# A decode step of attention and MLP on one core: x's load on another queue, two groups of loads merged, products in pairs, one semaphore for two copies

## The chip, the cores and the metric

The kernel runs on one core of one Trainium2 chip. The metric is the device time of one execution in microseconds (us). Three runs of the kernel before took 100.2, 100.45 and 100.91 us, median 100.45. Besides these there is one profiled execution.

## The reference

One token (x is one row of 1024 numbers, bf16) goes through a layernorm, and its result through two branches, which are added to x. Cut to what matters:

```python
xn = layernorm(x)
# branch A: attention of one query over the last W = 4096 positions of the cache
q = (xn @ wq).reshape(32 heads, 128)             # wq: 1024 x 4096
k, v = k_cache[:, -W:, :], v_cache[:, -W:, :]    # 4 heads x 4096 x 128, each serves 8 query heads
p = softmax(q @ k.T * 128**-0.5)
A = (p @ v).reshape(4096) @ wo                   # wo: 4096 x 1024
# branch B: an MLP with a layernorm of its own
y = layernorm(xn)
B = gelu(y @ w1 + b1) @ w2 + b2                  # w1: 1024 x 3584, w2: 3584 x 1024
out = x + A + B
```

In bf16 wq, wo are 8 MB each, w1 and w2 7 MB each, and the used parts of K and V 4 MB each: some 40 MB are read for one row of output.

## The kernel before, in words

All weights stream from HBM through four large SBUF buffers (slot 0 to 3, 32 KB in each of 128 partitions), in this order: wq's first row, K, the rest of wq, b1 and b2, w1, V, w2, wo. A "row" of a weight here is one step of the contraction: a weight of 1024 or 4096 or 3584 rows is laid over 128 partitions, and row c holds one 1024 (or 4096, 3584) long line for each partition. wo has 32 such rows of 2 KB per partition.

The order of the work is written by hand as a list of operations (class Plan). Each names an engine, what it reads and what it writes; `emit` (L27) works out from these keys which operation must wait for which, gives each engine's waited-for operations ticks of that engine's semaphore, gives every load a semaphore of its own, and puts the instructions out. SyncE (SP) issues all loads of the plan in list order, so a load that has to wait for its buffer holds back the ones behind it.

Before the plan come a few loads outside it (L205): SyncE issues wq's first row (1 MB) and then K in four loads, one for each of the four heads (`load_k`, L199; head g goes to partitions g, g+4, g+8, ...), and ACT issues the load of x, 2 KB, as a 32x32 tile x32. `tc.close()` then ends this part with a barrier over all engines (L209).

Then, in the order in which TensorE (PE) works:

- x: GpSimd (POOL) makes a mask (spread, L260, L261), and four small products with it bring x into a column layout (L284). The layernorms are short VectorE (DVE) operations, with two sums on TensorE (L286 to L316).
- K is transposed in 32x32 blocks on VectorE (four transposes, L340, which read all four heads), and copied into place by ACT (L345) and VectorE (L349).
- q = xn @ wq (L375 and helper L233), scores, w1's products, the softmax.
- V's products in a loop (L501), whose output is scaled and turned into o8, one column for each row of wo (L517 to L544).
- w2's rows go partly to VectorE (running sums in run, L488), and rows 21 to 27 to TensorE (`bulk_rows`, L528, into sc_ps).
- wo's rows 0 to 15 are loaded in two loads (L511, slot 0) and multiplied row by row: each row needs one weight load and two products of 512 columns, all into PSUM partition 0 of sc_ps. wo's rows 16 to 31 are loaded in pieces of 8, 4, 2, 1 and 1 rows (L513, slot 2). Rows 16 to 23 are multiplied in pairs (groups=2): two rows at once, in two column groups of the array, into partitions 0 and 32 of sc_ps.
- VectorE adds sc_ps to run (two halves, L556), while rows 24 to 31 go into another PSUM buffer (L567), to which run is added by small products (L572).
- VectorE and ACT each copy one part of the result (L575, L576), and SyncE and ACT each store one half (L578, L579). Each store needs both copies: it waits for VectorE's semaphore and for ACT's.

The rule that says for each row of wo which load it needs, and the calls that multiply them:

```python
return wo_t[i][:, r, :], f"wo0{r // 8 * 8}" if i == 0 else f"wo1{max(a for a in cuts if a <= r)}"
...
bulk_rows(list(range(16)), wo_row, ocol, "o8")
bulk_rows(list(range(16, NB)), wo_row, ocol, "o8", last=True, groups=2)
```

Of the kernel before, what the change touches and what calls it, by code (L numbers as in the profile page):

```python
# [14 lines left out]
class Plan:  # L15
# [8 lines left out]

        self.ops.append((eng, fn, tuple(r), tuple(w), dma, tuple(over)))

    def emit(self, done):  # L27
        nc, ops = self.nc, self.ops
        writer, readers, deps = {}, {}, []
        for n, (eng, fn, r, w, dma, over) in enumerate(ops):  # L30
# [26 lines left out]
        for n, (eng, fn, r, w, dma, _) in enumerate(ops):  # L57
            c, mine = clock[eng], []
# [13 lines left out]
        wanted = {m for mine in waits for m in mine if ops[m][4] is None}  # L72
        wanted.update(m for m in range(len(ops)) if m in done)
        sems = {e: nc.alloc_semaphore(f"{e}_count") for e in ("pe", "pool", "sp")}
        used, ends = list(sems.values()), []
        value, ticks = {}, {e: 0 for e in self.engines}
# [2 lines left out]
            ends.append(sems[e])  # L79
        left = nc.alloc_semaphore("left")  # L80
        ends.append(left)
        for n in done:
            value[n] = (nc.alloc_semaphore(f"dma{n}"), 16)
        for n, (eng, fn, r, w, dma, _) in enumerate(ops):
            if dma is not None:
                if n in done:
                    continue
                value[n] = (nc.alloc_semaphore(f"dma{n}") if dma is True else dma, 16)
                used.append(value[n][0])
            elif n in wanted:  # L90
                ticks[eng] += 1
                value[n] = (sems[eng], ticks[eng])

# [25 lines left out]
        for n in done:  # L119
            s, v = value[n]  # L120
# [18 lines left out]
def kernel(  # L139
# [32 lines left out]
    NB = 24  # L172
# [13 lines left out]
    slot = [sb(f"slot{i}", [P, 16384], BF16) for i in range(4)]  # L186
# [5 lines left out]

    x_flat = A_x.rearrange("a b d -> (a b d)")
    k_sb, kt_scr = slot[0], slot[3]
    k_sem = [nc.alloc_semaphore(f"k{g}") for g in range(Hkv)]
    wq_v = A_wq.rearrange("(p c) n -> p c n", p=P)
    wq_sem = nc.alloc_semaphore("wq0")

    def load_k(g):  # L199
        return nc.sync.dma_start(out=k_sb[g:P - Hkv + g + 1:Hkv, :],  # L200
                                 in_=A_k_cache[0, g, Sk - W:Sk, :].rearrange("(r c) d -> r (c d)", r=P // Hkv))

    x32 = sb("x32", [Hq, Hq], BF16)
    x_sem = nc.alloc_semaphore("x32")
    for i, sem in [(nc.sync.dma_start(out=slot[1][:, 0:NQ], in_=wq_v[:, 0, :]), wq_sem)] + [(load_k(g), k_sem[g]) for g in range(Hkv)] + [(nc.scalar.dma_start(out=x32, in_=x_flat.rearrange("(a j) -> a j", a=Hq)), x_sem)]:  # L205
        i.then_inc(sem, 16)
        tc.no_tile_sem_insts.add(i.ins.name)
    tc.close()
# [2 lines left out]
    plan = Plan(nc)  # L211
    pe, dve, act, pool, sp = nc.tensor, nc.vector, nc.scalar, nc.gpsimd, nc.sync

    def op(eng, fn, r=(), w=()):
        plan.add(eng, fn, r, w)

    def dma(eng, out_ap, in_ap, r=(), w=(), over=()):
        q = plan.engines[eng]
        plan.add(eng, lambda: q.dma_start(out=out_ap, in_=in_ap), r, w, True, over)  # L219
# [19 lines left out]
        op("pe", lambda: pe.matmul(out_ap, lhsT=w_ap, rhs=x_ap, start=start, stop=stop, tile_position=pos), r, w)  # L239

    plan.add("sp", lambda: None, (), ("wq0",), wq_sem)
    for g in range(Hkv):
        plan.add("sp", lambda: None, (), (f"k{g}",), k_sem[g])
    plan.add("act", lambda: None, (), ("x32",), x_sem)

    w1_v = B_w1.rearrange("(p c) n -> p c n", p=P)
    w2_v = B_w2.rearrange("(p c) n -> p c n", p=P)
# [89 lines left out]
    T5 = kt_scr.rearrange("p (s c a j) -> p s c a j", s=NS, a=4, j=32)  # L337
    T3 = kt_scr.rearrange("p (c a j) -> p c a j", a=4, j=32)
    for s in range(NS):
        op("dve", lambda s=s: dve.transpose(out=scr[:, s, :], in_=k2[:, s, :]), ("k0", "k1", "k2", "k3", "slot0"), (f"scr{s}",))  # L340
    pairs = [(R, Cd) for R in range(4) for Cd in range(4)]
    ACT_PAIRS = 6
    for s0, s1 in ((0, 1), (1, 2), (2, 4)):
# [39 lines left out]
    for c in (2, 3):  # L383
        for t in range(4):
            ldw(xw[:, 96 + P * c:97 + P * c], (0, 32 * t), ("xw",))
        for b in range(2):
            for t in range(4):
                j = 2 * (3 - t) + b
# [119 lines left out]
    op("pe", lambda: pe_loop("v", (NCH - 2) // UV, v_rows), v_in, ())  # L508
    op("pe", lambda: v_step(NCH - 1, False, True), v_in, ("qo",))
    wo_t = [slot[s].rearrange("p (r n) -> p r n", r=16) for s in (0, 2)]  # L510
    for a in (0, 8):  # L511
        dma("sp", wo_t[0][:, a:a + 8, :], wo_v[:, a:a + 8, :], (), (f"wo0{a}",), ("slot0",))
    cuts = [0, 8, 12, 14, 15, 16]  # L513
    for a, b in zip(cuts[:-1], cuts[1:]):
        dma("sp", wo_t[1][:, a:b, :], wo_v[:, 16 + a:16 + b, :], (), (f"wo1{a}",), ("slot2",))
# [31 lines left out]

    def wo_row(c):
        i, r = divmod(c, 16)
        return wo_t[i][:, r, :], f"wo0{r // 8 * 8}" if i == 0 else f"wo1{max(a for a in cuts if a <= r)}"  # L550

    ocol = lambda c: o8[:, c:c + 1]
    bulk_rows(list(range(16)), wo_row, ocol, "o8")
    bulk_rows(list(range(16, NB)), wo_row, ocol, "o8", last=True, groups=2)
    for half in range(2):
        op("dve", lambda half=half: dve.tensor_tensor(out=run[0][0:33, 512 * half:512 * half + 512], in0=bulk[:, half, :],  # L556
                                                      in1=run[0][0:33, 512 * half:512 * half + 512], op=ALU.add), ("bulk", "run0"), (f"sum{half}",))
# [19 lines left out]
    out_v = out.rearrange("a b (t s n) -> t (a b) s n", t=2, s=16)  # L577
    dma("sp", out_v[0], res[0:1, :].rearrange("a (s n) -> a s n", s=16), ("res_a", "res_b"), ("out0",))  # L578
    dma("act", out_v[1], res[32:33, :].rearrange("a (s n) -> a s n", s=16), ("res_a", "res_b"), ("out1",))  # L579
    plan.emit([len(plan.ops) - 2, len(plan.ops) - 1])  # L580


# [28 lines left out]
```

## Time and profile before

| what | value |
|---|---|
| three runs | 100.2, 100.45, 100.91 us |
| profiled execution, its own time | 99.88 us |
| its span, first to last instruction | 98.6 us |
| mean granted TensorE clock | 0.879 |
| busy: PE, DVE, ACT, POOL | 59.4, 73.9, 30.8, 10.0 us |
| SyncE's load queue: packets, MB | 3082, 39.86 |
| x's load on ACT's queue: issued, us to landing | 0.80, 3.4 |
| K's four loads: issued | 1.26, 1.84, 2.47, 3.10 |
| K's four loads: us to landing | 6.9, 8.7, 10.6, 12.3 |
| first transpose of K on VectorE starts | 15.48 |
| wo's rows 0 to 7 and 8 to 15: issued | 58.27, 58.64 |
| wo's rows 0 to 7 and 8 to 15: us to landing | 23.2, 27.8 |
| result copies start: DVE, ACT | 96.73, 96.83 |
| stores are issued: SP, ACT | 97.25, 97.27 |

How to read it: times inside the profile count from the span's start. "Issued" is when the engine's queue took the load, and "us to landing" counts from there until its semaphore was full, so a long time to landing is mostly a place far back in the queue. Engine names in the profile's lines: PE is TensorE, PEld its weight loads, DVE VectorE, POOL GpSimd, SP SyncE; L233 and L219 are lines of helpers that issue most products and all of the plan's loads. In lines of the timeline the bracket at the end is the idle time before the group and what ended it.

### The profile page before, as it was taken

How to read it: one execution, taken by the hardware profiler on the slowest of the kernel's cores; microseconds unless marked ns; L12 is line 12 of the kernel's file. 1: busy time of each engine (PE TensorE's matmuls, PEld its weight loads, DVE VectorE, ACT ScalarE, POOL GpSimd, SP SyncE). 2: the span in 40 equal slices, each digit the busy share in tenths (PEclk: the TensorE clock that was granted, in tenths of full speed). 3: DMA queues.
4: the chain of work that ended last, by engine and by line, in shares of the span. 5: the costliest groups of instructions: out<-in, count | busy, mean ns of one | idle time of the engine just before them, and what ended most of it. 6: DMA issues, size and time to landing. Idle time of an engine off the chain costs nothing.

```text
span 98.6 us, 958 instructions
## 1 busy us (share of the span) xinstructions
PE 59.4 (60%) x323; PEld 16.6 (17%) x220; DVE 73.9 (75%) x75; ACT 30.8 (31%) x29; POOL 10.0 (10%) x22
## 2 busy tenths in 40 slices
PE   0032040599400699940899566887671899995792
PEld 0022000123000234400212111212211111111130
DVE  0023777999999999999103685999999999999231
ACT  0050000089999899992002095000000000000001
POOL 0072580000000670000000000000000000000000
PEclk9999999999998558995559999579998558999999
DMA  2999979999999899899799999999998999999970
GB/s 60 443 442 439 479 316 475 425 525 425 425 425 404 384 407 512 384 407 512 311 425 425 425 437 434 419 425 459 430 489 371 432 425 445 432 425 382 401 288 1
DMA packets 3133, 39.86 MB, mean 404 GB/s; under 512 B 439, under 2 KB 445, under 8 KB 829
## 3 DMA queue, kind: packets, MB, share of 16 engines
q1 hardware_dynamic: 3082, 39.86, 95.5%
q10 hardware_dynamic: 50, 0.00, 0.0%
q14 instruction: 1, 0.00, 0.0%
HBM read 39.86 MB, written 0.00 MB: 404 GB/s over the span
## 4 chain that ended last, share of the span: by engine, by line
DMA 64%; PE 25%; issue 4%; SPq 1%; DVE 0%
DMA slot<-in_A_wq_dram 27%; DMA slot<-in_A_wo_dram 20%; DMA slot<-in_A_v_cache_dram 17%; PE qo_ps L501 11%; PE acc L375 10%; PE acc L233 2%; PE acc L239 1%; SPq L219 1%; DVE res L575 0%
## 5 line engine op out<-in xcount | busy, mean ns | idle before, releaser
L345 ACT COPY kT<-slot 32x1024 bf16<-32x1024 bf16 (+1 forms) x18 | 23.9, 1327 | 14.2 <-DVE slot L340 14.0
L488 DVE SCALAR_TENSOR_TENSOR run<-slot,hTf,run 128x1024 f32<-128x1024 bf16 x20 | 24.2, 1270 | 0.0
L375 PE MATMUL acc<-slot,xw 128*128 x48 | 16.1, 514 | 11.6 <-DMA slot<-in_A_wq_dram 11.6
L340 DVE STREAM_TRANSPOSE slot<-slot 128x4096 bf16<-128x4096 bf16 x4 | 17.4, 4413 | 1.1 <-DMA slot<-in_A_k_cache_dram 1.1
L501 PE MATMUL qo_ps<-slot,eTb 128*128 (+1 forms) x32 | 11.3, 436 | 4.2 <-issue 2.9
L349 DVE COPY kT<-slot 32x4096 bf16<-32x4096 bf16 x10 | 13.2, 1316 | 0.2
L233 PE MATMUL sc_ps<-slot,o 128*1 128x512 bf16 x48 | 9.1, 379 | 1.6 <-DMA slot<-in_A_wo_dram 1.6
L375 PEld LDWEIGHTS acc<-slot,xw 128*128 x48 | 5.7, 118 | 22.7 <-issue 20.2
L576 ACT CAST res<-acc 33x224 bf16<-33x224 f32 x1 | 0.3, 339 | 20.4 <-PE acc L233 20.4
L233 PE MATMUL sc_ps<-slot,hT 128*1 128x512 bf16 x14 | 6.0, 618 | 0.5 <-DMA slot<-in_B_w_dram 0.5
L233 PE MATMUL sc_ps<-kT,qm 128*32 128x512 bf16 x32 | 5.7, 914 | 0.3 <-DVE qm L422 0.3
L501 PEld LDWEIGHTS qo_ps<-slot,eTb 128*128 (+1 forms) x32 | 3.1, 98 | 12.1 <-issue 8.7
L544 ACT CAST o<-misc 128x32 bf16<-128x32 f32 x1 | 0.2, 187 | 14.6 <-PE misc L239 14.6
L434 DVE COPY sc<-sc_ps 128x512 f32<-128x512 f32 x1 | 0.7, 692 | 5.3 <-PE sc_ps L233 5.3
L225 PEld LDWEIGHTS <-o 128*1 128x1 bf16 x40 | 2.4, 85 | 11.6 <-issue 10.9
L239 PE MATMUL misc<-x,spread 32*128 32x8 bf16 x4 | 0.3, 168 | 6.2 <-POOL spread L261 6.2
L239 PE MATMUL acc<-spread,qm 32*128 32x512 bf16 x4 | 1.6, 497 | 3.7 <-POOL qm L321 3.7
L255 DVE MEMSET mhalf<- 128x1 f32 x1 | 0.1, 59 | 5.0 <-PEq L209 5.0
L233 PE MATMUL acc<-slot,yT 128*1 128x448 bf16 x64 | 3.5, 353 | 0.0
L433 ACT COPY sc<-sc_ps 128x512 f32<-128x512 f32 x1 | 0.6, 591 | 8.4 <-PE sc_ps L233 8.4
L239 PE MATMUL qo_ps<-selq,q_sb 128*128 128x4 bf16 x8 | 0.4, 169 | 4.0 <-DVE q_sb L394 4.0
L257 ACT ACT_TABLE_LOAD x1 | 1.3, 1283 | 4.8 <-PEq L209 4.8
(88 smaller groups left out, 48.1 us busy)
## 6 DMA issues: line engine op xcount, KB each, us to landing
slot<-in_B_w_dram SPq DMA_DIRECT2D x3, 3584.0 KB, 16.6
slot<-in_A_wo_dram SPq DMA_DIRECT2D x3, 2048.0 KB, 23.2
slot<-in_A_k_cache_dram SPq DMA_DIRECT2D x4, 1024.0 KB, 9.6
slot<-in_A_wq_dram SPq DMA_DIRECT2D x1, 4096.0 KB, 26.9
slot<-in_A_v_cache_dram SPq DMA_DIRECT2D x1, 4096.0 KB, 16.5
slot<-in_A_wq_dram SPq DMA_DIRECT2D x2, 1024.0 KB, 9.1
slot<-in_A_wq_dram SPq DMA_DIRECT2D x1, 2048.0 KB, 17.7
slot<-in_B_w_dram SPq DMA_DIRECT2D x1, 2048.0 KB, 21.5
```

The costliest lines, as they stand in the source:

```text
L219: plan.add(eng, lambda: q.dma_start(out=out_ap, in_=in_ap), r, w, True, over)
L225: return pe.add_instruction(mybir.InstLdweights(name=nc.get_next_instruction_name(), engine=i.engine, tile_size=(P, 32), tile_position=pos ...
L233: return pe.add_instruction(mybir.InstMatmult(name=nc.get_next_instruction_name(), engine=i.engine, start_tensor_calc=start, stop_tensor_c ...
L239: op("pe", lambda: pe.matmul(out_ap, lhsT=w_ap, rhs=x_ap, start=start, stop=stop, tile_position=pos), r, w)
L257: op("act", lambda: act.activation(out=dummy[:, 0:1], in_=mhalf[0:1, 0:1], func=ACT.Exp), ("mhalf",), ("act_warm",))
L340: op("dve", lambda s=s: dve.transpose(out=scr[:, s, :], in_=k2[:, s, :]), ("k0", "k1", "k2", "k3", "slot0"), (f"scr{s}",))
L345: op("act", lambda s0=s0, s1=s1, R=R, Cd=Cd: act.copy(out=kT[32 * Cd:32 * Cd + 32, R, s0:s1, :].rearrange("p s (c j) -> p (s c) j", j=32), ...
L349: op("dve", lambda R=R, Cd=Cd: dve.tensor_copy(out=kT[32 * Cd:32 * Cd + 32, R, :, :].rearrange("p s (c j) -> p (s c) j", j=32), in_=T3[32 ...
L375: pe.matmul(acc2[:, b, :], lhsT=xw[:, bass.ds(32 * n + 512 * i, P)], rhs=slot[1 + i][:, bass.ds(1024 * n + 512 * b, 512)], start=False, st ...
L434: op("dve", lambda: dve.tensor_copy(out=sc[:, 0:512], in_=sc_ps[:, 0, :]), ("sc0",), ("scs0",))
L488: op("dve", lambda: dve.scalar_tensor_tensor(out=t, in0=wap, scalar=hTf[:, c:c + 1], in1=t, op0=ALU.mult, op1=ALU.add), (key, "hTf", f"run ...
L501: return pe.matmul(qo_ps, lhsT=cols, rhs=v4[:, :, c, :], start=first, stop=last)
```

## The change

Four edits.

- The load of x is issued by SyncE, after wq's first row and ahead of K, and no longer by ACT.
- K is loaded by one load of 128 rows of 32 KB in place of four loads of 32 such rows. The layout in SBUF is the same: partition 4r + g holds piece r of head g. The transposes wait for one semaphore.
- wo's rows 0 to 15 come in one load of 32 KB per partition in place of two of 16 KB, and their products are made in pairs, in one run with those of rows 16 to 23. The weight loads and products are as many as before. All of rows 0 to 15 wait for the one load.
- The two result copies add to one new semaphore, "copied", and both stores wait for it to reach 2, in place of a wait for VectorE's and one for ACT's.

```diff
-    def emit(self, done):
+    def emit(self, done, last):
...
+        copied = nc.alloc_semaphore("copied")
+        ends.append(copied)
+        for n in last:
+            value[n] = (copied, len(last))
...
-            elif n in wanted:
+            elif n in wanted and n not in last:
...
-    k_sem = [nc.alloc_semaphore(f"k{g}") for g in range(Hkv)]
+    k_sem = nc.alloc_semaphore("k")
...
-    def load_k(g):
-        return nc.sync.dma_start(out=k_sb[g:P - Hkv + g + 1:Hkv, :],
-                                 in_=A_k_cache[0, g, Sk - W:Sk, :].rearrange("(r c) d -> r (c d)", r=P // Hkv))
+    k_rows = A_k_cache[0, :, Sk - W:Sk, :].rearrange("g (r c) d -> r g (c d)", r=P // Hkv)
...
-    for i, sem in [(nc.sync.dma_start(out=slot[1][:, 0:NQ], in_=wq_v[:, 0, :]), wq_sem)] + [(load_k(g), k_sem[g]) for g in range(Hkv)] + [(nc.scalar.dma_start(out=x32, in_=x_flat.rearrange("(a j) -> a j", a=Hq)), x_sem)]:
+    for i, sem in [(nc.sync.dma_start(out=slot[1][:, 0:NQ], in_=wq_v[:, 0, :]), wq_sem), (nc.sync.dma_start(out=x32, in_=x_flat.rearrange("(a j) -> a j", a=Hq)), x_sem), (nc.sync.dma_start(out=k_sb, in_=k_rows), k_sem)]:
...
-    for a in (0, 8):
-        dma("sp", wo_t[0][:, a:a + 8, :], wo_v[:, a:a + 8, :], (), (f"wo0{a}",), ("slot0",))
+    dma("sp", wo_t[0], wo_v[:, 0:16, :], (), ("wo0",), ("slot0",))
...
-        return wo_t[i][:, r, :], f"wo0{r // 8 * 8}" if i == 0 else f"wo1{max(a for a in cuts if a <= r)}"
+        return wo_t[i][:, r, :], "wo0" if i == 0 else f"wo1{max(a for a in cuts if a <= r)}"
...
-    bulk_rows(list(range(16)), wo_row, ocol, "o8")
-    bulk_rows(list(range(16, NB)), wo_row, ocol, "o8", last=True, groups=2)
+    bulk_rows(list(range(NB)), wo_row, ocol, "o8", last=True, groups=2)
...
-    plan.emit([len(plan.ops) - 2, len(plan.ops) - 1])
+    end = len(plan.ops)
+    plan.emit([end - 2, end - 1], [end - 4, end - 3])
```

More of the change, by code (lines that the diff above doesn't have):

```diff
@@ L241 @@
     plan.add("sp", lambda: None, (), ("wq0",), wq_sem)
-    for g in range(Hkv):
-        plan.add("sp", lambda: None, (), (f"k{g}",), k_sem[g])
-    plan.add("act", lambda: None, (), ("x32",), x_sem)
+    plan.add("sp", lambda: None, (), ("k",), k_sem)
+    plan.add("sp", lambda: None, (), ("x32",), x_sem)
     w1_v = B_w1.rearrange("(p c) n -> p c n", p=P)
@@ L339 @@
     for s in range(NS):
-        op("dve", lambda s=s: dve.transpose(out=scr[:, s, :], in_=k2[:, s, :]), ("k0", "k1", "k2", "k3", "slot0"), (f"scr{s}",))
+        op("dve", lambda s=s: dve.transpose(out=scr[:, s, :], in_=k2[:, s, :]), ("k", "slot0"), (f"scr{s}",))
     pairs = [(R, Cd) for R in range(4) for Cd in range(4)]
```

## The prediction, made before the changed kernel had run

> **What bounds the kernel now.** I read the page first (span, DMA row, queues), then the chain of waits, then the timeline of the end, then the DMA issues one at a time, and last the stretches with TensorE's granted clock.
>
> ```profile
> span 98.6 us, 958 instructions
> ...
> DMA  2999979999999899899799999999998999999970
> GB/s 60 443 442 439 479 316 475 425 525 425 425 425 404 384 407 512 384 407 512 311 425 425 425 437 434 419 425 459 430 489 371 432 425 445 432 425 382 401 288 1
> ...
> q1 hardware_dynamic: 3082, 39.86, 95.5%
> ```
>
> One queue, SyncE's, keeps the transfer engines busy from the first slice to the last but one. 39.86 MB at some 425 GB/s is 93.8 us, nearly the whole span. No wait of SyncE lets the queue run dry: v is issued at 43.02, while w1's second half lands only at 32.93 + 16.6 = 49.53. So the end follows the bytes, and after them a short tail. The chain says the same:
>
> ```profile
> 5.62 26.91 DMA slot<-in_A_wq_dram
> ...
> 43.02 16.51 DMA slot<-in_A_v_cache_dram
> ...
> 74.24 19.55 DMA slot<-in_A_wo_dram
> ...
> 96.41 0.30 PE acc L233 x2
> 96.71 0.02 issue
> 96.73 0.45 DVE res L575
> ```
>
> The last load (wo's row 31, issued 75.66, 20.7 us to landing) lands at 96.36, and its products start at 96.41. The tail is 0.3 us of products, 0.45 of copy, the store. In the timeline the stage that the change touches reads:
>
> ```profile
> 76.66 5.96 PE L233 MATMUL sc_ps<-slot,hT 128*1 128x512 bf16 x14 [0.48 <-DMA slot<-in_B_w_dram]
> ...
> 82.46 3.62 PE L233 MATMUL sc_ps<-slot,o 128*1 128x512 bf16 x16
> ...
> 86.45 3.61 PE L233 MATMUL sc_ps<-slot,o 128*1 128x512 bf16 x16 [0.37 <-DMA slot<-in_A_wo_dram]
> ...
> 91.34 1.89 PE L233 MATMUL sc_ps<-slot,o 128*1 128x512 bf16 x16 [1.27 <-DMA slot<-in_A_wo_dram]
> ...
> 93.27 1.28 DVE L556 TENSOR_TENSOR run<-sc_ps,run 33x512 f32<-33x512 f32 x2 [1.82 <-PE sc_ps L233]
> ```
>
> wo's rows 0 to 7 start at 82.46, rows 8 to 15 wait for their load until 86.45, rows 16 to 23 (already in pairs) until 91.34. TensorE waits for data each time; it has 1.27 us to spare before row 16.
>
> **The change part by part.**
>
> K in one load. From issue plus time to landing, K's four loads land at 1.26 + 6.9 = 8.16, 10.54, 13.07 and 3.10 + 12.3 = 15.40: 7.24 us for three, so 9.65 for four. The nearest single load of 128 rows of 32 KB is wq's last (from 5.14 + 17.7 = 22.84 to 5.62 + 26.9 = 32.52), 9.68 us for the same 4 MB. Gain 0, ends -0.1 and +0.1. All four heads were needed for the first transpose (15.48) before too. SyncE's issues shrink from 2.45 us to about 0.4, so the start barrier that opens the engines' programs at 4.75 may open some 1.5 us sooner; that buys nothing, as wq's next loads only queue behind K (13.2 us from issue to landing) and GpSimd's masks then wait for x.
>
> One rule speaks against this part. K's four heads lie 16 MiB apart, and the new load takes a row of each in turn; v's load reads its four heads in just that way and takes 59.52 - 49.53 = 9.99 us for its 4 MB, 420 GB/s, which its rows of 8 KB explain (wq's load of that row size: 17.95 - 15.40 = 2.55 per MB, 10.2 for four). So from rows nothing is lost. The Trainium skill ("DMA: Bandwidth & Descriptors", Latency and other measured facts) says that rows spaced by a large power of two fall to 103 GB/s at a pitch of 4 or 8 MiB; by that figure K would take 40.7 us, an estimate from that page, and the end would come 31 us later; v's row disagrees with it here. It stays as a rival.
>
> x on SyncE behind wq's first row. That load lands at 0.80 + 5.0 = 5.80, and loads of this queue land in order. Two tiny loads (b1 and b2) took 32.67 - 32.52 = 0.15 us of the queue together, so x lands near 5.9. Its first reader, TensorE, was held until 6.19 by GpSimd's mask; with an earlier barrier it waits for x instead, at about the same time. Behind that: the layernorm chain on VectorE ends at 14.40 and K's first transpose waits until 15.48, so 1.07 us of lateness is free. On the queue x costs 0 to 0.15 us more, but its packets ran on the same engines before, on ACT's queue. Could the start gain? First bytes move at 1.8; from 2.0 to 2.6 only 123 GB/s move, just when x's small packets run. If wq's first row went like K's first load (2.36 us) with the 0.7 us that the very last bytes needed to be signalled, it would land at 4.86, not 5.80. So the ends are -0.94 and +0.15. I take 0: nothing ties the slow start to x rather than to the start of the queue itself.
>
> wo's rows 0 to 15 in one load. Before, 76.6 (w2's last landing) to 81.47 to 86.44: 4.87 + 4.97 = 9.84 us. As one load of 32 KB rows, 9.68 by wq's row. So -0.16, with ends -0.3 (one load less to signal besides) and 0. It moves every later landing, so it reaches the end.
>
> The wait that this adds: row 0 now waits for the whole load, until about 86.2 + 0.05, not 82.46. Behind it on TensorE stand all the products up to the last. In the pairs' favour: rows 16 to 23 step by 0.433 us a pair (weight loads at 91.56, 91.98, 92.42, 92.85), the single rows by 0.43 each. So 16 rows take 8 x 0.433 = 3.46 us instead of 7.2 and are through at 89.7, before row 16's load (91.1). Cost 0, hidden by that wait, if the clock is full.
>
> But TensorE now idles from 82.3 to 86.25, and the clock column says what idling has done:
>
> ```profile
> 73.00:74.00 1.00, 0.84 (x3) 0.22 (x3) 1.00 (x2) 0.00 (x0) 0.00 (x0) 1.00 1.00 430
> 74.00:75.00 1.00, 0.00 (x0) 0.00 (x0) 0.96 (x2) 0.00 (x0) 0.00 (x0) 1.00 1.07 459
> 75.00:76.00 1.00, 0.10 (x4) 0.11 (x4) 0.97 (x3) 0.00 (x0) 0.00 (x0) 0.75 0.65 274
> 76.00:77.00 1.00, 0.52 (x5) 0.15 (x4) 1.00 (x2) 0.19 (x1) 0.00 (x0) 0.50 0.96 410
> 77.00:78.00 1.00, 1.00 (x4) 0.23 (x2) 1.00 (x2) 0.00 (x0) 0.00 (x0) 0.50 1.00 426
> ```
>
> (The third number from the end is the clock; my first column of busy time is TensorE's.) After 73.87 TensorE idles, at 75.5 the clock halves, at 82.25 it is full again, and in between the rows of w2 step by 0.853 us (77.04, 77.90, 78.75). In finer stretches the changes stand at 31.1, 37.9, 44.8, 51.6, 61.9, 65.35, 75.5 and 82.25: all on a grid of about 3.42 us. Down after a grid interval with under half of it busy, up after a nearly full one; 74% busy (75.5 to 78.9) was not enough. So an idle stretch of 3.95 us holds more than half of some interval, and the clock will fall. The cost depends on where the grid lies: with c us at half clock the 16 rows take 3.46 + 0.49c. From row 16's start to row 31's products it is at least 4.58 us: 1.89 of products, 1.28 of VectorE's two additions, 0.13 of hand-overs, 0.65 of run's products, 0.63 of rows 28 to 30. Row 31 lands at 96.41 - 0.20 = 96.21, so the end is delayed only if the 16 rows are through later than 91.63. With c = 3.41 (one interval) they are through at 91.4: hidden. With c from 4.6 to 6.3 (the rest of one interval and another) at 92.0 to 92.8: the end comes 0.2 to 1.0 us later than before, load gain included. The two are about equally likely by the grid's place. I take 0, with ends 0 and +1.2. The Trainium skill ("TensorE: Matmul & The Clock Gate", Part 1: The HAM clock gate) has a free-running window of 3413 ns, which agrees with the grid, and a clock that falls after at least one idle window; that trace is harsher, 1.6 us of idling sufficed at 75.5. By that page's idle window alone the clock still falls for most places of the grid, so it changes no sum.
>
> One semaphore for the two result copies. VectorE's copy ends at 97.18, ACT's at 97.17, the stores issue at 97.25 and 97.27. One wait less on each of the two queues: pieces of about 0.05 us in the chain. -0.04, ends -0.08 and 0.
>
> Sum: 0 (K) + 0 (x) - 0.16 (wo's load) + 0 (pairs) - 0.04 (semaphore) = -0.20 us. Against the profiled execution, 99.88 us (98.6 of span and 1.28 around it), 99.68. The median of the three runs shown is 0.57 higher, so 100.25 us.
>
> **The rivals.** A is the sum: 100.25, own range 99.9 to 100.6.
>
> B, slower: the halved clock outlasts the slack. Place: the 16 rows after 86.25; it decides once they are through after 91.63, that is with more than about 3.9 us at half clock. Price +0.2 to +1.0 against before, 100.65 to 101.45, in the middle 101.0. For it: every idle stretch over 1.7 us before a grid point in the trace but the one at 27.7. Against: half of the grid's places leave c at 3.41 or less.
>
> C, faster: the slow start was x's. Up to -0.94 on top of A: 99.3 to 100.0. For it: 123 GB/s just after 2.0. Against: a queue's first load may ramp so by itself.
>
> D: K's rows 16 MiB apart slow its load. At the lowest rate that the trace has under load, 123 GB/s, K takes 34.1 us instead of 9.65: +24.5, 125 us. Against it: v's row.
>
> F, slower: x's landing is late. It decides when x comes 2.9 us after 6.19: 1.07 before K's transpose and 1.82 before VectorE's addition at 93.27. If it came with K's end, 15.40, the end would move by 15.40 - 6.19 - 2.9 = 6.3 us, to 106.5. Against: landings in order.
>
> **How the numbers follow.** A 0.43, B 0.33, C 0.14, D 0.02, F 0.08. About 1% (1.0 us) is what a measurement of this kernel can tell from no change. Faster by more: C's larger half, 0.09. Slower by more: B's top 0.06, D 0.02, F 0.08: 0.16. Within 1%: A 0.43, B 0.27, C 0.05: 0.75. The range holds A, nearly all of B and half of C: 99.6 to 101.3 us; what it leaves out is D, F, the far ends of B and C, near 0.2.
>
> **What would show it.** K lands in one piece near 15.4; x near 5.9, and VectorE's first transpose starts at 15.3 to 15.6. wo's first load lands 9.7 us after w2's last; then eight pairs, at 0.433 us (A) or first 0.853 (B), and before row 16 TensorE waits for a load (A) or not (B). VectorE's additions then start at 93.1 (A) or 93.8 and later (B). wq's first row landing before 5.3 shows C. I am wrong if the loads after K land at another pace, if TensorE's clock stays full through the idle stretch, or if the last product no longer waits for the last load.

## The result, and the profile after

| | before | after |
|---|---|---|
| median of six runs, us | 100.08 (99.72 to 100.91) | 101.9 (100.9 to 103.05) |
| ratio, 95% interval | 1 | 1.016 [1.0128, 1.0193] |
| profiled execution, us | 99.88 | 102.82 |
| its span, us | 98.6 | 101.4 |

The changed kernel is 1.6% slower. I had forecast 100.25 us in a range of 99.6 to 101.3: the time is outside it, on the slow side. The ratio leaves out two of the six runs, 102.82 and 103.05 us, as more than 1.5% above the fastest, and the profiled execution is the first of them. The spans of the changed kernel are 99.5 to 101.4, median 100.3, so the profile's +2.8 us of span is more than the typical +1.8, and it has to be split with care.

The page of the kernel after, its first lines of the transfer engines and queue:

```profile
span 101.4 us, 950 instructions
...
DMA  2999999999999899999999999999999999999900
GB/s 48 440 327 414 414 417 411 453 491 414 453 453 406 385 441 441 464 419 396 381 433 414 420 454 415 436 482 391 453 441 412 427 465 388 433 391 420 362 23 1
...
q1 hardware_dynamic: 2938, 39.86, 93.3%
```

The same bytes flow through the same queue, and still without a pause. One slice stands out: the third (5.1 to 7.6 us) moves 327 GB/s, where before it moved 442. That is where K begins. A closer look is a pair of stretches, 6 to 9 us, first of the kernel before, then of the kernel after (the last number is GB/s, the one before it the share of the transfer engines' time, and before that stands TensorE's clock; ahead of it the busy us of PE, PEld, DVE, ACT and POOL, each with its number of instructions):

```profile
6.00:9.00 3.00, 1.38 (x8) 1.18 (x8) 1.11 (x7) 0.24 (x2) 1.22 (x8) 1.00 1.17 502
```

```profile
6.00:9.00 3.00, 1.42 (x8) 1.19 (x8) 1.11 (x8) 0.00 (x0) 0.21 (x2) 1.00 0.90 350
```

152 GB/s less for 3 us is 0.46 MB less, which at 425 GB/s is 1.07 us of the queue's time. In the records of single packets K's 32 KB rows take 1.213 us each before; after, 18 of the first 32 take more than 1.32 us and up to 2.06, and those that start after 8 us are near 1.21 again. The loss is uneven: the first of K's 16 completion signals comes 0.78 us later than before (15.56, before 14.78), the last 1.74 us later, and a load has landed only with the last.

The DMA issues of the kernel after (the last column is us from issue to landing), and in its timeline the first reader of K, with the same line of the kernel before behind it:

```profile
slot<-in_A_k_cache_dram SPq DMA_DIRECT2D x1, 4096.0 KB, 15.5
...
slot<-in_A_wo_dram SPq DMA_DIRECT2D x1, 4096.0 KB, 28.2
...
slot<-in_A_wo_dram SPq DMA_DIRECT2D x2, 256.0 KB, 20.6
x<-in_A_x_dram SPq DMA_DIRECT2D x1, 2.0 KB, 4.7
```

```profile
1.27 0.40 SPq L207 DMA_DIRECT2D x<-in_A_x_dram  x1
1.72 0.64 SPq L207 DMA_DIRECT2D slot<-in_A_k_cache_dram  x1
3.38 1.29 SPq L221 DMA_DIRECT2D slot<-in_A_wq_dram  x3
...
17.22 4.45 DVE L341 STREAM_TRANSPOSE slot<-slot 128x4096 bf16<-128x4096 bf16 x1 [2.92 <-DMA slot<-in_A_k_cache_dram]
```

```profile
15.48 4.45 DVE L340 STREAM_TRANSPOSE slot<-slot 128x4096 bf16<-128x4096 bf16 x1 [1.07 <-DMA slot<-in_A_k_cache_dram]
```

x lands at 1.27 + 4.7 = 5.97, in time. K lands at 1.72 + 15.5 = 17.2, where before its last piece landed at 15.45: +1.7. From there every load keeps that lateness. (Landings from here on are the last completion signal of the load; a sum of issue and rounded time to landing, as in the prediction, can be off by 0.1.)

| landing, us | before | after | difference |
|---|---|---|---|
| wq's first row | 5.75 | 5.80 | 0 |
| K (last piece) | 15.45 | 17.20 | +1.7 |
| wq, last | 32.53 | 34.30 | +1.8 |
| w2, last | 76.62 | 78.34 | +1.7 |
| wo's rows 0 to 15, all | 86.41 | 88.06 | +1.7 |
| wo's row 31 | 96.36 | 98.00 | +1.6 |

It is the stream itself that is late, and not a load that had to wait for the work behind K: v, for one, is issued at 44.65, while the load ahead of it lands only at 51.31.

The chain of waits now goes through K:

```profile
1.72 15.47 DMA slot<-in_A_k_cache_dram
...
17.22 17.44 DVE slot L341 x4
...
59.85 28.21 DMA slot<-in_A_wo_dram
...
88.11 8.24 PE sc_ps L235 x48
...
99.56 0.45 DVE res L574
```

And the end, in the timeline of the kernel after:

```profile
88.11 8.24 PE L235 MATMUL sc_ps<-slot,o 128*1 128x512 bf16 x48 [3.90 <-DMA slot<-in_A_wo_dram]
88.49 0.13 PEld L227 LDWEIGHTS <-o 128*1 128x1 bf16 x2 [4.57 <-issue]
89.34 0.13 PEld L227 LDWEIGHTS <-o 128*1 128x1 bf16 x2 [0.72 <-issue]
...
94.24 0.09 PEld L227 LDWEIGHTS <-o 128*1 128x1 bf16 x2 [0.51 <-issue]
94.68 0.09 PEld L227 LDWEIGHTS <-o 128*1 128x1 bf16 x2 [0.34 <-issue]
...
96.39 1.28 DVE L555 TENSOR_TENSOR run<-sc_ps,run 33x512 f32<-33x512 f32 x2 [3.23 <-PE sc_ps L235]
...
99.56 0.45 DVE L574 CAST res<-acc 33x288 bf16<-33x288 f32 x1 [1.90 <-PE acc L235]
```

The pairs step by 0.85 us (88.49, 89.34) until the clock is full again at 94.0, and by 0.44 after that. They have no wait for row 16's load left, and VectorE's additions start at 96.39 where they started at 93.27. The last product no longer waits for the last load: res starts 99.56 - 98.00 = 1.56 us after it, before 96.73 - 96.36 = 0.37. So of the span's +2.83 us, 1.64 is late loads and 1.19 is TensorE at half clock. These are the shares of this one execution. The second part does not come in every run, as the experiments show; how large the first is in the other five isn't on record, but the shortest of the six spans is still 1.0 us over the median before, 98.5.

### The profile page after: what moved, and what is told of

Its sections match the earlier page's. It is cut to its first block, busy times and chain, and to the rows that moved or that the text cites. A ratio compares the mean times of both kernels' runs of the same rounds, so it can differ in the third digit from the quotient of the medians.

```text
span 101.4 us, 950 instructions
## 1 busy us (share of the span) xinstructions
PE 58.3 (58%) x323; PEld 16.2 (16%) x220; DVE 74.0 (73%) x75; ACT 30.8 (30%) x29; POOL 9.9 (10%) x22
## 4 chain that ended last, share of the span: by engine, by line
DMA 43%; DVE 33%; PE 19%; SPq 1%; issue 1%; ACT 1%; DVEq 0%
DMA slot<-in_A_wo_dram 28%; DVE slot L341 17%; DMA slot<-in_A_k_cache_dram 15%; PE sc_ps L235 14%; DVE kT L350 13%; PE acc L235 3%; PE acc L241 1%; DVE m_loc L442 1%; SPq L207 1%; DVE q_sb L395 1%; ACT sc L434 1%; DVE res L574 0%; PE misc L241 0%; PE qo_ps L241 0%; DVE m_row L446 0%
## 5 line engine op out<-in xcount | busy, mean ns | idle before, releaser
L235 PE MATMUL sc_ps<-slot,o 128*1 128x512 bf16 x48 | 8.2, 523 | 3.9 <-DMA slot<-in_A_wo_dram 3.9
L376 PEld LDWEIGHTS acc<-slot,xw 128*128 x48 | 5.6, 117 | 24.5 <-issue 22.3
L555 DVE TENSOR_TENSOR run<-sc_ps,run 33x512 f32<-33x512 f32 x2 | 1.3, 678 | 3.2 <-PE sc_ps L235 3.2
## 6 DMA issues: line engine op xcount, KB each, us to landing
slot<-in_A_k_cache_dram SPq DMA_DIRECT2D x1, 4096.0 KB, 15.5
```

Source lines behind the costliest of these rows:

```text
L235: return pe.add_instruction(mybir.InstMatmult(name=nc.get_next_instruction_name(), engine=i.engine, start_tensor_calc=start, stop_tensor_c ...
L376: pe.matmul(acc2[:, b, :], lhsT=xw[:, bass.ds(32 * n + 512 * i, P)], rhs=slot[1 + i][:, bass.ds(1024 * n + 512 * b, 512)], start=False, st ...
```

## The experiments

My theory after this comparison: x's short load, where it now stands in SyncE's queue, slows K's first rows. Rivals: K's one load does it (rows of four heads in turn), or the idle clock alone makes the difference. Ratios are to the kernel before on the same chip, with the 95% interval; landings are of the one execution that was profiled, the span is the median of all runs.

| run | edit | ratio | K landed | last load landed | median span |
|---|---|---|---|---|---|
| before | | 1 | 15.45 | 96.36 | 98.5 (96 runs, 98.3 to 99.1) |
| after | all four | 1.016 [1.0128, 1.0193] | 17.20 | 98.00 | 100.3 |
| e1 | after, K in four loads | 1.0128 [1.0082, 1.0174] | 16.61 | 97.42 | 100.05 |
| e2 | after, x by ACT | 1.0065 [1.0033, 1.0098] | 15.12 | 96.60 | 99.45 |
| e3 | after, wo as before | 1.0082 [1.0049, 1.0115] | 16.45 | 97.42 | 99.5 |
| e4 | before, K in one load, copied | 1.0037 [0.9999, 1.0074] | 15.35 | 96.36 | 98.95 |
| e5 | before, x by SyncE | 1.0129 [1.0089, 1.0169] | 16.70 | 97.56 | 99.7 |
| e6 | before, wo's part | 1.0028 [0.9992, 1.0064] | 15.21 | 96.15 | 98.7 |

### One part undone (e1, e2, e3)

e1 puts the four loads of K back, e2 has x issued by ACT again, e3 has the two loads and single rows of wo.

e1, against the kernel after:

```diff
-    for i, sem in [(nc.sync.dma_start(out=slot[1][:, 0:NQ], in_=wq_v[:, 0, :]), wq_sem), (nc.sync.dma_start(out=x32, in_=x_flat.rearrange("(a j) -> a j", a=Hq)), x_sem), (nc.sync.dma_start(out=k_sb, in_=k_rows), k_sem)]:
+    for i, sem in [(nc.sync.dma_start(out=slot[1][:, 0:NQ], in_=wq_v[:, 0, :]), wq_sem), (nc.sync.dma_start(out=x32, in_=x_flat.rearrange("(a j) -> a j", a=Hq)), x_sem)] + [(load_k(g), k_sem[g]) for g in range(Hkv)]:
...
-        op("dve", lambda s=s: dve.transpose(out=scr[:, s, :], in_=k2[:, s, :]), ("k", "slot0"), (f"scr{s}",))
+        op("dve", lambda s=s: dve.transpose(out=scr[:, s, :], in_=k2[:, s, :]), ("k0", "k1", "k2", "k3", "slot0"), (f"scr{s}",))
```

e2, against the kernel after:

```diff
-    for i, sem in [(nc.sync.dma_start(out=slot[1][:, 0:NQ], in_=wq_v[:, 0, :]), wq_sem), (nc.sync.dma_start(out=x32, in_=x_flat.rearrange("(a j) -> a j", a=Hq)), x_sem), (nc.sync.dma_start(out=k_sb, in_=k_rows), k_sem)]:
+    for i, sem in [(nc.sync.dma_start(out=slot[1][:, 0:NQ], in_=wq_v[:, 0, :]), wq_sem), (nc.scalar.dma_start(out=x32, in_=x_flat.rearrange("(a j) -> a j", a=Hq)), x_sem), (nc.sync.dma_start(out=k_sb, in_=k_rows), k_sem)]:
```

e3, against the kernel after:

```diff
-    dma("sp", wo_t[0], wo_v[:, 0:16, :], (), ("wo0",), ("slot0",))
+    for a in (0, 8):
+        dma("sp", wo_t[0][:, a:a + 8, :], wo_v[:, a:a + 8, :], (), (f"wo0{a}",), ("slot0",))
...
-    bulk_rows(list(range(NB)), wo_row, ocol, "o8", last=True, groups=2)
+    bulk_rows(list(range(16)), wo_row, ocol, "o8")
+    bulk_rows(list(range(16, NB)), wo_row, ocol, "o8", last=True, groups=2)
```

Expected of e1:

> The changed kernel with K in four loads again; x stays on SyncE ahead of K, and wo's part stays changed. In the changed kernel K landed at 17.2 us where it was 15.4, and every later load was 1.6 to 1.8 late. Theory K (the one load of all four heads is itself slower): K's last piece lands near 15.5, wo's last row near 96.3, and the time is within 0.5 us of the kernel before where TensorE's clock is kind, up to 1.2 above it where not: ratio 1.000 to 1.010. Theory x (x's small packets ahead of K upset the queue): K stays near 17.2 and the ratio near 1.016.

Expected of e2:

> The changed kernel with x's load on ACT's queue again; K stays in one load, and wo's part stays changed. Theory K: K still lands near 17.2, the ratio stays 1.012 to 1.020. Theory x: K lands near 15.4 and the ratio falls to 1.000 to 1.010.

Expected of e3:

> The changed kernel with wo's rows 0 to 15 in two loads and multiplied row by row again; K's, x's and the semaphore's edits stay. Both theories of the start: K lands near 17.2 and the last load near 98.1. Theory of the clock: with the idle stretch gone TensorE waits for the loads again, so the end follows the last load by 2.2 us in every run, times spread by less than 1 us and none is over 102.0; ratio 1.012 to 1.020. If instead the pairs and the one load had cost most of the 1.6%, the ratio falls below 1.008.

Only e2 brings K back to 15.1 and the last load to within 0.24 us of before. With K in four loads (e1) K is still 1.2 us late. So x carries most of the lateness; K's merge and wo's part have smaller shares. e1 and e3 came out between the numbers of their theories: K at 16.61 and 16.45, where 15.5 or 17.2 was expected, and e3's times spread by 2.3 us in place of under 1. One of e3's twelve spans is 98.4, as short as before's, with x still on SyncE.

e1 and e2 also show the half clock in executions of ordinary length. In e2 the clock is at half from 85.24 to 92.07, and the products start at 86.70:

```profile
86.70 7.97 PE L235 MATMUL sc_ps<-slot,o 128*1 128x512 bf16 x48 [6.53 <-DMA slot<-in_A_wo_dram]
```

e2's span ends 3.09 us after its last landing and e1's 2.91 us, where before's ends 2.23 us after it. With wo as before (e3) it is 2.18 us.

### One part alone (e4, e5, e6)

e4 takes over the diff's lines of K and of the copied semaphore (x stays with ACT), e6 those of wo. e5, against the kernel before:

```diff
-    for i, sem in [(nc.sync.dma_start(out=slot[1][:, 0:NQ], in_=wq_v[:, 0, :]), wq_sem)] + [(load_k(g), k_sem[g]) for g in range(Hkv)] + [(nc.scalar.dma_start(out=x32, in_=x_flat.rearrange("(a j) -> a j", a=Hq)), x_sem)]:
+    for i, sem in [(nc.sync.dma_start(out=slot[1][:, 0:NQ], in_=wq_v[:, 0, :]), wq_sem), (nc.sync.dma_start(out=x32, in_=x_flat.rearrange("(a j) -> a j", a=Hq)), x_sem)] + [(load_k(g), k_sem[g]) for g in range(Hkv)]:
```

The core of e4 and of e6, against the kernel before:

```diff
-    for i, sem in [(nc.sync.dma_start(out=slot[1][:, 0:NQ], in_=wq_v[:, 0, :]), wq_sem)] + [(load_k(g), k_sem[g]) for g in range(Hkv)] + [(nc.scalar.dma_start(out=x32, in_=x_flat.rearrange("(a j) -> a j", a=Hq)), x_sem)]:
+    for i, sem in [(nc.sync.dma_start(out=slot[1][:, 0:NQ], in_=wq_v[:, 0, :]), wq_sem), (nc.scalar.dma_start(out=x32, in_=x_flat.rearrange("(a j) -> a j", a=Hq)), x_sem), (nc.sync.dma_start(out=k_sb, in_=k_rows), k_sem)]:
```

```diff
-    for a in (0, 8):
-        dma("sp", wo_t[0][:, a:a + 8, :], wo_v[:, a:a + 8, :], (), (f"wo0{a}",), ("slot0",))
+    dma("sp", wo_t[0], wo_v[:, 0:16, :], (), ("wo0",), ("slot0",))
...
-    bulk_rows(list(range(16)), wo_row, ocol, "o8")
-    bulk_rows(list(range(16, NB)), wo_row, ocol, "o8", last=True, groups=2)
+    bulk_rows(list(range(NB)), wo_row, ocol, "o8", last=True, groups=2)
```

Expected of e4:

> The kernel before with K in one load and the one semaphore for the result copies, and nothing else: x on ACT, wo in two loads, row by row. Theory K: K lands near 17.2, the last load is 1.6 to 1.8 us late, ratio 1.014 to 1.020. Theory x: K lands near 15.4, ratio 0.997 to 1.003.

Expected of e5:

> The kernel before with one edit: x's load on SyncE, behind wq's first row and ahead of K's four loads. So far x on SyncE went with ratios of 1.013 and 1.008 and with K and everything behind it 1.0 to 1.8 us late, where x on ACT had K at 15.1 to 15.4. Theory x (a tiny load in SyncE's queue at the start delays the stream behind it): K's last piece lands at 16.3 or later, ratio 1.006 to 1.012. Theory 'x only together with another edit': K lands by 15.6, ratio 0.998 to 1.003.

Expected of e6:

> The kernel before with wo's part alone: rows 0 to 15 in one load, products in pairs. Theory of the clock: last load lands near 96.2, and the end follows it by 2.2 us when TensorE's clock is full in time and by up to 1.2 more when not: times from 99.7 to 101.2 in one group of runs and ratio 1.002 to 1.007. If wo's part is free, ratio 0.996 to 1.000, no run over 100.6.

e5 settles it: x's place alone costs 1.3%, 101.18 us against 99.95. Its stretch from 6 to 9 us looks like that of after, and its first transpose starts at 16.72:

```profile
6.00:9.00 3.00, 0.93 (x7) 0.76 (x7) 1.11 (x7) 0.69 (x2) 1.66 (x8) 1.00 0.85 339
```

```profile
1.26 0.40 SPq L205 DMA_DIRECT2D x<-in_A_x_dram  x1
1.72 2.43 SPq L200 DMA_DIRECT2D slot<-in_A_k_cache_dram  x4
...
16.72 4.45 DVE L340 STREAM_TRANSPOSE slot<-slot 128x4096 bf16<-128x4096 bf16 x1 [1.88 <-DMA slot<-in_A_k_cache_dram]
```

e4 falls into two groups: six runs with spans of 98.3 to 98.7, as before, and six of 99.2 to 99.8. Its profile is of the first group and shows no late landing; the longer group has none.

e6 falls into two groups as well, and these are the two cases of my forecast. Six spans are 98.3 to 98.5, up to 0.2 us under before's 98.5, and six are 98.9 to 99.6. Its profile, of the first group, shows the clock falling and yet no loss: the products are through before row 31 is there, and VectorE's additions start at 93.05 (before 93.27):

```profile
86.23 6.78 PE L233 MATMUL sc_ps<-slot,o 128*1 128x512 bf16 x48 [3.78 <-DMA slot<-in_A_wo_dram]
...
93.05 1.28 DVE L554 TENSOR_TENSOR run<-sc_ps,run 33x512 f32<-33x512 f32 x2 [1.79 <-PE sc_ps L233]
...
96.52 0.45 DVE L573 CAST res<-acc 33x288 bf16<-33x288 f32 x1 [2.19 <-PE acc L233]
```

The stretches around it give the length of the half clock:

```profile
85.00:86.00 1.00, 0.00 (x0) 0.00 (x0) 1.00 (x2) 0.00 (x0) 0.00 (x0) 0.77 0.85 361
86.00:87.00 1.00, 0.77 (x4) 0.13 (x2) 1.00 (x2) 0.00 (x0) 0.00 (x0) 0.50 1.00 426
87.00:88.00 1.00, 1.00 (x8) 0.13 (x2) 1.00 (x2) 0.00 (x0) 0.00 (x0) 0.50 1.12 475
88.00:89.00 1.00, 1.00 (x8) 0.13 (x2) 1.00 (x2) 0.00 (x0) 0.00 (x0) 0.52 0.88 377
89.00:90.00 1.00, 1.00 (x12) 0.24 (x6) 1.00 (x1) 0.00 (x0) 0.00 (x0) 1.00 1.08 459
```

It falls at about 85.5 and is full again at about 89.0: some 2.7 us of it after the products start at 86.23, under the 3.9 us from which I had it decide. In the profile of after it is 94.0 - 88.11 = 5.9 us, over it, and the end moved.

### What it is about x's load (e7, e8, e9, e10, e12, e14)

In these x's own load stays with ACT, except in e10, and a second load that no operation uses stands in SyncE's queue: in e7 another 2 KB copy of x (32 rows of 64 bytes) between wq's first row and K, in e8 the same spread over partitions 0, 4, ..., 124, in e12 at that place 64 KB in 128 rows of 512 bytes. In e14 the 2 KB stand after K's first load, in e9 between K's third and fourth. e10 has x itself as SyncE's very first load, ahead of wq's first row. e7, against the kernel before; the transposes of K wait for xd's semaphore too, so the load is surely done:

```diff
+    xd = sb("xd", [P, Hq], BF16)
+    xd_sem = nc.alloc_semaphore("xd")
...
-    for i, sem in [(nc.sync.dma_start(out=slot[1][:, 0:NQ], in_=wq_v[:, 0, :]), wq_sem)] + [(load_k(g), k_sem[g]) for g in range(Hkv)] + [(nc.scalar.dma_start(out=x32, in_=x_flat.rearrange("(a j) -> a j", a=Hq)), x_sem)]:
+    for i, sem in [(nc.sync.dma_start(out=slot[1][:, 0:NQ], in_=wq_v[:, 0, :]), wq_sem), (nc.sync.dma_start(out=xd[0:Hq, :], in_=x_flat.rearrange("(a j) -> a j", a=Hq)), xd_sem)] + [(load_k(g), k_sem[g]) for g in range(Hkv)] + [(nc.scalar.dma_start(out=x32, in_=x_flat.rearrange("(a j) -> a j", a=Hq)), x_sem)]:
```

In e8 out is xd[0:P:4, :]. In e12 xd has 256 columns, and the load is (nc.sync.dma_start(out=xd, in_=wq_v[:, 0, 0:256]), xd_sem). The line of e14, then that of e9, then that of e10:

```python
    for i, sem in [(nc.sync.dma_start(out=slot[1][:, 0:NQ], in_=wq_v[:, 0, :]), wq_sem)] + [(load_k(g), k_sem[g]) for g in range(1)] + [(nc.sync.dma_start(out=xd[0:Hq, :], in_=x_flat.rearrange("(a j) -> a j", a=Hq)), xd_sem)] + [(load_k(g), k_sem[g]) for g in range(1, Hkv)] + [(nc.scalar.dma_start(out=x32, in_=x_flat.rearrange("(a j) -> a j", a=Hq)), x_sem)]:
...
    for i, sem in [(nc.sync.dma_start(out=slot[1][:, 0:NQ], in_=wq_v[:, 0, :]), wq_sem)] + [(load_k(g), k_sem[g]) for g in range(3)] + [(nc.sync.dma_start(out=xd[0:Hq, :], in_=x_flat.rearrange("(a j) -> a j", a=Hq)), xd_sem), (load_k(3), k_sem[3])] + [(nc.scalar.dma_start(out=x32, in_=x_flat.rearrange("(a j) -> a j", a=Hq)), x_sem)]:
...
    for i, sem in [(nc.sync.dma_start(out=x32, in_=x_flat.rearrange("(a j) -> a j", a=Hq)), x_sem), (nc.sync.dma_start(out=slot[1][:, 0:NQ], in_=wq_v[:, 0, :]), wq_sem)] + [(load_k(g), k_sem[g]) for g in range(Hkv)]:
```

Expected of e7:

> The kernel before with a second load of x (2 KB, 32 rows of 64 bytes, to partitions 0 to 31 of a tile that nothing uses) on SyncE between wq's first row and K; x itself stays on ACT. Theory x as a tiny load in the queue: same as with x there, K at 16.3 or later, ratio 1.006 to 1.012. If it was not the load but its absence from ACT's queue, or when the layernorm chain starts: K by 15.6 and 0.998 to 1.003.

Expected of e8:

> As the run with the second tiny load, but its 32 rows go to partitions 0, 4, 8, ... 124. If what hurts is that the tiny rows of all engines are written to one corner of SBUF, K lands by 15.6 and the ratio is 0.998 to 1.004. If any tiny load at this place hurts, K is at 16.3 or later and the ratio 1.006 to 1.012.

Expected of e9:

> The kernel before with the second tiny load of x on SyncE, now between K's third and fourth load, when the stream has been running for 8 us. If a tiny load hurts wherever it stands in the queue, K's fourth load and all behind it come 0.6 to 1.2 us late, ratio 1.006 to 1.012. If it hurts only while the stream starts, K lands by 15.6 and the ratio is 0.999 to 1.004. The loads of b1 and b2 stand in the queue of the kernel before at 32.5 us; there the spread of the later landings stayed what it was, which speaks for the second.

Expected of e10:

> The kernel before with x's load on SyncE as its very first, ahead of wq's first row, and none on ACT. SyncE's later issues move by one issue, 0.46 us. If only a tiny load between big ones hurts: wq's first row lands 0 to 0.5 later than 5.8, K at 15.4 to 15.9, ratio 1.000 to 1.005. If x must not be on this queue at all: K at 16.3 or later, ratio 1.008 or more.

Expected of e12:

> As the run with a second tiny load between wq's first row and K, but with 128 rows of 512 bytes (64 KB) instead of 32 rows of 64 bytes. Its bytes cost 0.15 us at 425 GB/s. If rows of 64 bytes are what hurts: K at 15.5 to 15.8, ratio 1.000 to 1.004. If any short load at this place does: K at 16.3 or later, ratio 1.007 to 1.014.

Expected of e14:

> The second tiny load of x on SyncE between K's first and second load. Between wq's first row and K it cost 0.9%, between K's third and fourth nothing. If what is sensitive is the change from wq's short rows to K's long ones, nothing here: K at 15.5, ratio 0.999 to 1.003. If it is the time since the start (until about 8 us): K at 16 or later, ratio 1.004 to 1.010.

| run | the short load | ratio | GB/s, 6 to 9 us | K landed | last load landed |
|---|---|---|---|---|---|
| before | none | 1 | 502 | 15.45 | 96.36 |
| e7 | 2 KB, ahead of K | 1.009 [1.0061, 1.012] | 426 | 16.27 | 97.20 |
| e8 | the same, spread | 1.010 [1.0063, 1.0136] | 415 | 16.09 | 96.98 |
| e12 | 64 KB in rows of 512 bytes | 1.0099 [1.006, 1.0139] | 350 | 16.60 | 97.52 |
| e14 | 2 KB, after K's first load | 1.0002 [0.9986, 1.0019] | 525 | 15.33 | 96.26 |
| e9 | 2 KB, after K's third load | 1.000 [0.9976, 1.0025] | 513 | 15.34 | 96.27 |
| e10 | x first of all | 1.0043 [1.0016, 1.0069] | 393 | 15.77 | 96.77 |

The stretch that tells most is e14's, with the same number of loads and bytes as e7:

```profile
6.00:9.00 3.00, 0.85 (x6) 0.68 (x6) 1.11 (x7) 0.76 (x2) 1.73 (x8) 1.00 1.23 525
```

Of the places tried, a short load costs 0.9 to 1.3% at one only, between the first megabyte and K. One load later it costs nothing. (Of the 50 runs with a short load at the costly place, in after, e1, e3, e5, e7, e8 and e12, one escaped, the 98.4 of e3.) That x no longer came by ACT isn't it (e7 leaves it there), nor the partitions it goes to (e8), nor rows as short as 64 bytes (e12). e10 pays 0.4%, about its one issue of 0.46 us ahead of all other loads: its last load lands 0.41 us late. What slows K's first rows there isn't shown: the packet records show them slow, not why. e14's short packets run at 7.3 to 7.6 us and e7's at 4.7 to 5.1, so the sensitive thing can be the change from wq's rows of 8 KB to K's of 32 KB, or the first 5 us as such; no run tells these apart.

### K's rows (e15)

```diff
-    k_rows = A_k_cache[0, :, Sk - W:Sk, :].rearrange("g (r c) d -> r g (c d)", r=P // Hkv)
+    k_rows = A_k_cache[0, 0, Sk - Hkv * W:Sk, :].rearrange("(p c) d -> p (c d)", p=P)
```

e15 is e4 with 128 rows that lie behind one another (16384 positions of one head in place of the last 4096 of four), so its scores are those of other positions.

Expected of e15:

> K's one load and the one semaphore alone, as in the run with K only (ratio 1.0037, 5 of 12 runs over 100.6), but the 128 rows of 32 KB are read from one place (the last 16384 positions of head 0), not from four heads 16 MiB apart: the scores are those of other positions. If the four heads' distance makes K's load slower: ratio 0.997 to 1.002 and at most 1 run in 10 over 100.6. If one load in place of four does: ratio 1.002 to 1.007 and a third or more of the runs over 100.6.

0.9993 [0.9973, 1.0012], all twelve spans between 98.4 and 98.7. The long group of e4 is gone. It's one load of the same size, and the start barrier opens early in both (e4 2.92, e15 2.45), so what made half of e4's runs 1 us longer goes with where the rows lie. Two doubts are left: e4 and e15 ran on two different chips, each against the kernel before on its own, and K's issue takes SyncE 0.64 us in e4 and 0.41 in e15. The packets speak for the rows: even in e4's profile, of the shorter group, 7 of K's first 32 rows take more than 1.32 us, up to 1.84; in e15's all take 1.213. (The stretch of 6 to 9 us says less: 470 GB/s in e4's profile and 513 in e15's, but 470 also in e6's, where K is as before.)

### The clock kept full (e11, e13)

Both are e6 with extra products of one row of w2 in TensorE's idle stretch, whose result is thrown away: 20 in a row in e11, a loop of four times four in e13 (which has the copied semaphore too). What e11 adds to e6:

```diff
+    ldw(hcol(21), (0, 0), ("hT",))
+    for u in range(20):
+        mm(misc[0:1, :], hcol(21), w2_row(21)[0][:, 0:512], True, True, (0, 0), (w2_row(21)[1],), ("misc",))
```

Expected of e11:

> The kernel before with wo's part (one load, pairs), and 20 more products on TensorE between the last row of w2 and the first of wo, on data that is there, into PSUM that nobody reads: some 4.3 us at full clock, so that TensorE does not idle while it waits for wo's load. Their result is thrown away. Theory of the clock: the clock stays full from w2's rows to the end, the pairs step by 0.43 us, TensorE waits for row 16's load, the end follows the last load by 2.2 us in every run: times 99.5 to 100.2 (without the 100.3 to 101.9 that wo's part alone had in 8 of 12 runs), ratio 0.995 to 0.999. If the clock was not the cause, times as with wo's part alone, ratio 1.001 to 1.006.

Expected of e13:

> wo's part and the one semaphore on the kernel before (x on ACT, K in four loads), with the filling products now in a loop of 4 turns with 4 products each, so that TensorE's program grows by 9 instructions and not 21. Their result is thrown away. In the run with 21 more, the clock stayed full and the pairs stepped by 0.43 us as the theory of the clock has it, but a 16 KB load of instructions ran in the middle of V's load, one transfer engine came 1.4 us late and stayed so, and the ratio was 1.0095. Theory of the clock, with that instruction load as the only spoiler: no such load here, last load at 96.2, times 99.5 to 100.1, ratio 0.995 to 0.999. If filling products cost by themselves, or the clock was not the cause: ratio 1.002 or more.

e6 has seven of its twelve times from 100.3 to 101.9, not eight as the first of these says, and six long spans. The timeline of e13:

```profile
81.33 3.62 PE L559 MATMUL misc<-slot,hT 128*1 128x512 bf16 x16
86.33 3.62 PE L237 MATMUL sc_ps<-slot,o 128*1 128x512 bf16 x32 [1.39 <-DMA slot<-in_A_wo_dram]
...
91.23 1.89 PE L237 MATMUL sc_ps<-slot,o 128*1 128x512 bf16 x16 [1.29 <-DMA slot<-in_A_wo_dram]
```

With the idle stretch filled the clock is full from 81.2 on, the first 16 rows take 3.62 us where after's 24 took 8.24, TensorE waits for row 16's load again, and all six spans lie between 98.3 and 98.8: e6's long group is gone. So within the span the theory of the clock holds. By device time neither kernel wins; of both I expected 0.995 to 0.999. e13 takes 101.75 us, 1.0193 [1.0163, 1.0224]: its time outside the span is 3.2 to 3.8 us, that of before on the same chip 1.5 in the median; what that time is isn't shown. e11 takes 1.0095 [1.0061, 1.013]: its last load lands 1.4 us late. V is the first load to be late: its landing spreads over 2.0 us (59.01 to 60.99) between the first transfer engine and the last, before over 0.6. Its page has a row that before lacks:

```profile
q8 instruction: 1, 0.02, 0.1%
```

That one packet of 16 KB runs at 53.8 us on a transfer engine in the middle of V. e2, e3, e5 and e13 have the row too, but there the packet comes at 97.7 to 99.2, after the last load. That it delays e11's engine is likely by its place and time; I did not test it.

## Why the prediction was wrong, step by step

**x behind wq's first row: the step that failed.** I took 0, with +0.15 as the worst end. Measured: +1.2 us alone (e5), 0.9 to 1.0% for a bare copy of the load (e7, e8). That it is x's load at this place is shown; why it slows K's first rows stays open. The price came from b1 and b2, two small loads in the middle of the stream, 0.15 us together. That row was right for its place, the middle of the stream, as e9 shows (and e14, already one load later), but x's place is another one: behind the first load of the queue and ahead of the first big rows. I searched that place only for a gain (C) and for x's own landing (F), and looked at the bytes x adds rather than at the load behind it. wq's first row landed at 5.80, so C's gain wasn't there, and x at 5.97, so F's loss wasn't either.

**K in one load: the term was too small.** 0 with ends of 0.1 either way became +0.37% [-0.01, +0.74] in e4, about 0.4 us on average, as no cost in half the runs and 1 us in the other half. So rival D was right in kind, and its price of 24.5 us was far off. My evidence was v's load, which reads four heads in turn at 420 GB/s; it ran in the middle of the stream. The Trainium skill ("DMA: Bandwidth & Descriptors", Latency and other measured facts) warns of rows spaced by large powers of two, with 103 GB/s at 4 and 8 MiB, measured on copies between HBM tensors in rows of 16 KiB. The runs agree with its direction, as e15 removes the cost, and not with a rate like that: even in after, where x also weighs on it, K's 4 MB took 17.20 - 5.97 = 11.2 us, 373 GB/s. The earlier barrier (3.38 in place of 4.75; 2.45 in e15, whose time is that of before) bought nothing, as forecast.

**wo's one load: right in sign, half as large.** -0.16 was forecast. From w2's last landing to that of wo's row 15 before takes 9.79 us, after and e6 9.72: -0.07. All other runs with two loads take 9.77 to 9.80, all with one load 9.71 to 9.73. The method was right: the row that I took it from, wq's last load, takes 9.72 too when its landings are read from the completion signals, so the error is that of rounded times (my 9.84 and 9.68). In e6 the last load lands at 96.15, 0.21 us sooner, but 0.15 of that is there already when w2 lands.

**Pairs and the idle clock: right as a mechanism, and B was no rarity.** The clock fell in the idle stretch, the pairs stepped by 0.853, and the loss depends on how much half clock is left after the load. e6's two groups are A (up to -0.2 us) and B (+0.4 to +1.1 us against before's 98.5; I had +0.2 to +1.0), six runs each; no execution of the longer group was profiled, but e13, with the clock kept full, has no such group. In the profiled execution of after B costs 1.19 us, at my upper end of +1.2. The mean over e6 is +0.28% [-0.08, +0.64]. In after, with x's and K's lateness, undoing wo's part (e3) brings 0.8%. The Trainium skill ("TensorE: Matmul & The Clock Gate", Part 1: The HAM clock gate) gives a free-running window of 3413 ns; after's clock changes at 76.95, 83.77, 87.19 and 94.01 stand one or two such steps apart, which agrees. By the Trainium skill's idle window alone my forecast had the clock fall "for most places of the grid"; that is wrong, as an idle stretch of 3.95 us holds a whole window of 3.41 only at (3.95 - 3.41) / 3.41 = 16% of the places, an estimate from the Trainium skill's figure. The runs needed less than a whole idle window: from 83.77 to 87.19 in after TensorE was still busy for 13% of the time, and the clock fell.

**One semaphore: right, and too small to time.** In after VectorE's copy ends at 100.01 and the stores issue at 100.04 and 100.05: 0.03 us where before it was 0.07. -0.04 was forecast for this step. e15, which has it too, takes 0.9993 [0.9973, 1.0012], so no gain shows in the time.

The parts alone add to 1.3 + 0.4 + 0.3 = 2.0%, against 1.6% [1.28, 1.93] together: within their intervals they add. My sum of -0.20 us held only its two small gains. B was my only way to a loss of a moderate size, and the range's upper end came from it. The base flatters the forecast, too: it was the median of three runs, 100.45, and six runs have 100.08, so the change itself was missed by 2.0 us (-0.20 against +1.82) and not by the 1.65 between 100.25 and 101.9. No version that I ran beats the kernel before beyond its interval.

## What to carry to other kernels

When one queue is the bound, price a moved load by what it does to the load behind it, and at its own place in the stream: a row from the steady stream did not hold for the first microseconds here, and no run made up a delay from there. In this kernel a short load belongs on another queue, or behind the first big load, not between the first load and the next. Merging two loads of 2 MB gained 0.07 us here, so look first at what the engine that waits for them then idles: at which point of TensorE's clock steps the data come was chance, so the change made two groups of runs, and the mean had to pay for the worse one.

## What the runs showed of the hardware that I had not expected

- 2 KB in SyncE's queue between the first megabyte and K's rows take 1 us from the whole stream (1.009 [1.0061, 1.012]); the same 2 KB one load later take nothing (1.0002 [0.9986, 1.0019]). Why is open.
- A lag between the transfer engines stays. In after K's 16 completion signals spread over 1.64 us, and those of wo's row 31, 80 us later, over 1.54; before it is 0.67 and 0.57. A load has landed only with the last of them. That it is the same engine each time is likely, but the records don't name it.
- A load of 128 rows taken from four heads in turn made two groups of runs, 1 us apart; the same load from one place made one (on another chip of the same kind).
- In e11 one instruction packet of 16 KB in mid-stream went with an engine 1.4 us late to the end, and e13, with its loop, spent 2 us more outside the span. Neither cause is shown.
